# Attention scores: masks, scale and row minimum of the negated scores in one VectorE instruction per 128 columns, in place of two instructions per 512

## The chip, the cores and the metric

One Trainium2 chip, one core of it. The time is that of one execution on the device in microseconds (us); the kernel before was timed in three runs, and one more execution of it was profiled. Lower is better.

## What is computed

Three layers in a row: attention with a local window and global tokens, a gated feed-forward layer, and a soft mixture of experts. All data is float32. The change touches the first layer only, and there the local queries:

```python
def _attn_ref(q_l, k_l, v_l, q_g, k_g, v_g):          # B, H, Sl, D = 4, 8, 512, 64; Sg = 32
    pos = np.arange(Sl)
    window, scale = 32, 1.0 / np.sqrt(D)
    k_all = np.concatenate([k_g, k_l], axis=2)
    v_all = np.concatenate([v_g, v_l], axis=2)
    s_g = scale * np.matmul(q_g, k_all.transpose(0, 1, 3, 2))
    out_g = np.matmul(sm(s_g), v_all)                  # sm: softmax over the last axis, with its max taken off
    s_ll = scale * np.matmul(q_l, k_l.transpose(0, 1, 3, 2))
    mask = np.abs(pos[:, None] - pos[None, :]) <= window
    s_ll = np.where(mask, s_ll, -1e9)
    s_lg = scale * np.matmul(q_l, k_g.transpose(0, 1, 3, 2))
    a_l = sm(np.concatenate([s_lg, s_ll], axis=-1))
    out_l = np.matmul(a_l, np.concatenate([v_g, v_l], axis=2))
    return np.concatenate([out_g, out_l], axis=2)
```

Then `x = (silu(x @ w_gate) * (x @ w_val)) @ w_out`, and a soft mixture of eight experts of four slots each over the 2176 tokens.

## The kernel before

**Tiling of the attention.** A block of 32 local queries sees at most three blocks of 32 keys and the 32 global keys, so a window of 128 keys. `kS` holds the keys so that each window is 128 columns in a row. The work is cut into 16 units `u`: eight groups `n` of four heads (a batch and half of its heads), each in two parts `tp` of 256 queries. In one unit `stage_scores` (L328) does two halves `hp`. A half is eight matmuls (L342) into one PSUM tile `sc` of 128 partitions x 4 pieces `bp` x 128 columns: a row is one query of one head, and a piece is its window. Then VectorE works on the whole tile of 512 columns: one SCALAR_TENSOR_TENSOR (L351) multiplies by the scale and adds `masks`, into the SBUF tile `sm`, and one TENSOR_REDUCE (L355) takes the maximum of each row of each piece, negated, into the four columns of `nm`:

```python
nc.vector.scalar_tensor_tensor(
    out=sm, in0=sc, scalar=SCALE, in1=masks[:, 4 * tp : 4 * tp + 4],
    op0=ALU.mult, op1=ALU.add,
)
nc.vector.tensor_reduce(
    out=d["nm"][:, hp], in_=sm, op=ALU.max, axis=AX.X, negate=True
)
```

`stage_exp` (L359) runs one ScalarE instruction per piece (L363): exp of `sm` with the column of `nm` as bias, into `p`, and the sum of the row out of ScalarE's accumulator into `rs`. The accumulator is read by an instruction of its own, ACTIVATION_READ_ACCUMULATOR.

**The masks** are built once at the start: two triangles `tri` by GpSimd (L277, L281), filled with `NEG` = -1e9 outside, copied to the places of `masks`, and two memsets (L309, L311).

**The order of the work** is written out by hand: the kernel turns the scheduler off, so every engine does its instructions in the order of the program. The loop over `u` (L511) issues, in this order: the scores of `u`; `split_rest` (the low part of an earlier unit's output, L405 on VectorE); one piece of the preparation of the next layer's weights (`prep_some`, L137 to L157 on VectorE, from u = 5 on); the transposes `ppT` of `p` of unit u-1 on TensorE (L372) and their copy `pT` by ScalarE (L375); the exps of `u`. For tp = 0 follow the scores of the global queries `gs`, `gt` (L445), their maximum (L449 to L452) and exps (L458 to L465); for tp = 1 the transposes `pg` of `pG` (L475). Then `stage_pv` of u-1: `o` (L386), 1/sum (L393, L394) and the product `xn` (L396). For tp = 1 the second half of `pg` and its copy `pGT` by VectorE (L479). For tp = 0 `stage_gpv` of n-1: `og` (L491), the sums (L496 to L498) and `xg` (L503). For tp = 1 `turn_v` of n+1: three GpSimd copies (L248 to L250) that make two of the three orders of the values, `vB` and `vC`, out of `vA`. Then `stage_xT` of u-2 (L419, and its copy L403 by ScalarE). At the end of a tp = 0 step SyncE issues the loads of the next group's values (`load_v`, L228 on); they write the buffers that `og` and `o` of the group before have read, so they wait for these.

**Buffers around the change.** The scores, and the global scores, take turns in three PSUM buffers (`ps_sc`); `sm` has two buffers, one per half, so the scores of a unit are worked on when the exps of the unit before have read theirs.

After the attention the same weights' preparation goes on beside the gated layer (L587 on), which is a long row of matmuls, and the mixture of experts follows.

Of the kernel before, what the change touches and what calls it, by code (L numbers as in the profile page):

```python
# [12 lines left out]
ALU = mybir.AluOpType  # L13
AX = mybir.AxisListType
PSUM = bass.MemoryType.PSUM

NEG = -1e9
# [19 lines left out]
def window(i):  # L37

    if i == 0:
        return 0, "A", 0  # L40
    m, k = divmod(i - 1, 3)
    return (4 * m, 4 * m + 2, 4 * m + 3)[k], "ABC"[k], m
# [3 lines left out]
def attention_moe_soft_moe_kernel(  # L46
# [15 lines left out]
    nc = tc.nc  # L62
# [6 lines left out]
    SCALE = 1.0 / float(D) ** 0.5  # L69
# [124 lines left out]
    masks = ast.tile([P, 8, P], F32, name="masks")  # L194
# [57 lines left out]
    def spread_q(n, a, eng, xs=slice(0, 16)):  # L252

        rows = slice(64 * a, 64 * a + 64)
        dst = qB[n % 2][rows].rearrange("p (a x g) -> p a x g", a=2, g=64)[
            :, :, xs, 32 * a : 32 * a + 32
        ]
        src = qT[n][rows].rearrange("p a (x q) -> p a x q", q=32)[:, :, xs]
        if eng is nc.scalar:
            nc.scalar.activation(dst, src, AF.Copy)  # L260
        else:
            eng.tensor_copy(dst, src)
# [7 lines left out]
    for _ in range(2):  # L270
# [5 lines left out]

    nc.gpsimd.affine_select(  # L277
        out=tri[:, 0], in_=tri[:, 0], pattern=[[1, 32]], compare_op=ALU.is_ge,
        fill=NEG, base=0, channel_multiplier=-1,
    )  # L280
    nc.gpsimd.affine_select(  # L281
        out=tri[:, 1], in_=tri[:, 1], pattern=[[-1, 32]], compare_op=ALU.is_ge,
        fill=NEG, base=0, channel_multiplier=1,
    )
    nc.gpsimd.memset(qB[0], 0.0)
    warm = ast.tile([1, 1], F32, name="warm")
# [2 lines left out]
    for g in (0, 1, 3, 2):  # L289
        bl = g // 2  # L290
        eng = nc.gpsimd if g == 3 else nc.vector
        if g == 2:
            spread_q(0, 0, nc.vector, slice(0, 8))
            for a, x0 in ((1, 0), (1, 8), (0, 8)):
                spread_q(0, a, nc.scalar, slice(x0, x0 + 8))
        rows = masks[32 * g : 32 * g + 32]
        for r in range(3):
            first = next(i for i in range(1, 16) if i % 3 == r and i % 2 == bl)
            p0 = first // 2
            n = len(range(p0, 8, 3))  # L300
            k = window(first)[1]
            for a, slot in ((0, {"A": 1, "B": 0, "C": 0}[k]), (1, 3)):
                eng.tensor_copy(
                    rows[:, p0 :: 3, 32 * slot : 32 * slot + 32],
                    tri[:, a].unsqueeze(1).to_broadcast([32, n, 32]),
                )
        if bl == 0:
            eng.tensor_copy(rows[:, 0, 64:96], tri[:, 1])
            eng.memset(rows[:, 0, 96:128], NEG)  # L309
        else:  # L310
            eng.memset(rows[:, 7, 96:128], NEG)  # L311
    nc.gpsimd.memset(qgB, 0.0)
    make_identity(nc, ident)
    for a in range(2):
        rows = slice(64 * a, 64 * a + 64)
# [12 lines left out]
    def stage_scores(u):  # L328
        n, tp = units[u]
        st[u] = d = {  # L330
            "p": [awk.tile([P, 4, P], F32, tag=f"p{a}", name=f"p{u}_{a}") for a in range(2)],
            "rs": awk.tile([P, 4, 2], F32, tag="rs", name=f"rs{u}", bufs=4),
            "nm": awk.tile([P, 2, 4], F32, tag="nm", name=f"nm{u}"),
            "sm": [awk.tile([P, 4, P], F32, tag="sm", name=f"sm{u}_{a}") for a in range(2)],
        }
        qb = qB[n % 2].rearrange("p (a x g) -> p a x g", a=2, g=64)
        for hp in range(2):
            sc = ps_sc.tile([P, 4, P], F32, tag="sc", name=f"sc{u}_{hp}")
            for i in range(8):
                blk = 8 * tp + i  # L340
                s0 = window(blk)[0]
                nc.tensor.matmul(  # L342
                    sc[64 * (i % 2) : 64 * (i % 2) + 64, i // 2],
                    qb[:, hp, blk],
                    kS[n][:, hp, 32 * s0 : 32 * s0 + 128],
                    start=True, stop=True, skip_group_check=True,
                )
            if hp == 0 and tp == 1:
                split_rest()
            sm = d["sm"][hp]  # L350
            nc.vector.scalar_tensor_tensor(  # L351
                out=sm, in0=sc, scalar=SCALE, in1=masks[:, 4 * tp : 4 * tp + 4],
                op0=ALU.mult, op1=ALU.add,
            )
            nc.vector.tensor_reduce(  # L355
                out=d["nm"][:, hp], in_=sm, op=ALU.max, axis=AX.X, negate=True
            )

    def stage_exp(u):  # L359
        d = st[u]  # L360
        for hp in range(2):
            for bp in range(4):
                nc.scalar.activation(  # L363
                    d["p"][hp][:, bp], d["sm"][hp][:, bp], AF.Exp,
                    bias=d["nm"][:, hp, bp : bp + 1], accum_out=d["rs"][:, bp, hp : hp + 1],
                )

    def stage_pT(u, hp):
# [39 lines left out]
    def split_rest():  # L408
        while rest:
            rest.pop(0)()  # L410
# [100 lines left out]
    for u in range(NU):  # L511
        n, tp = units[u]
        stage_scores(u)
        split_rest()
        prep_some()
        if u >= 1:
            stage_pT(u - 1, 0)
            stage_pT(u - 1, 1)
        stage_exp(u)
        if tp == 1 and n + 2 < NQ:  # L520
            load_k(n + 2)
# [32 lines left out]
    for a in range(4):  # L554
        rows = slice(32 * a, 32 * a + 32)
        nc.gpsimd.tensor_copy(istack[rows], ident[rows, rows])
    nc.gpsimd.memset(isel, 0.0)
    for a in range(2):
        rows = slice(64 * a, 64 * a + 64)
# [108 lines left out]
    nm = tpool.tile([P, 4, 4], F32, name="nm")  # L668
# [228 lines left out]
    base = S1 * NFC  # L897
# [106 lines left out]
    d, a, b, top, turned, tokens, sums, NJ = part_end(2, Ls, [Ls], [place["rB"]])  # L1004
# [93 lines left out]
    for e in range(E):  # L1098
# [8 lines left out]
        out=lr, in0=lr, in1=rc[:, 0].unsqueeze(2).to_broadcast([P, NK * 4, NS]), op=ALU.subtract  # L1107
# [6 lines left out]
        out=lr, in0=lr, in1=rc[:, 1].unsqueeze(2).to_broadcast([P, NK * 4, NS]), op=ALU.mult  # L1114
    )
    nc.vector.transpose(
        out=cT.rearrange("p k n -> p (k n)"), in_=Lr.rearrange("p k n -> p (k n)")
# [151 lines left out]
```

## Time and profile before

| | us |
|---|---|
| median of three runs | 548.22 |
| lowest and highest of the three | 546.24, 549.87 |
| the profiled execution | 550.9 |
| span of its trace | 549.1 |
| TensorE busy in the span | 502.9 (92%) |
| VectorE busy | 327.6 (60%) |
| ScalarE busy | 182.8 (33%) |
| GpSimd busy | 83.4 (15%) |

The profile is of one execution. Its span is the time from the first to the last instruction; the 1.8 us between the span and the execution's own time lie around it. Busy time is a mean over stages which differ; the attention takes about the first 135 us.

In the profile PE is TensorE, PEld its weight loads, DVE VectorE, ACT ScalarE, POOL GpSimd, SP SyncE. A row of a timeline gives the start, the duration, the engine, the line, the operation, what it writes and reads, and shapes as partitions x elements.

### The profile page before, as it was taken

To read this page: it belongs to the slowest core of one execution; us is meant where nothing else is said; L and a number is where in the kernel's file an instruction comes from. 1 tells how busy PE (TensorE), PEld (TensorE's weight loads), DVE (VectorE), ACT (ScalarE), POOL (GpSimd) and SP (SyncE) were. 2 spreads that over 40 slices of the span, in tenths; PEclk is the share of its full clock that TensorE was granted. 3 is DMA by queue.
4 is the path that set the end of the run, shared out by engine and by line. 5 is a ranking of instruction groups with operands and counts; after the bars stand their busy time and mean duration, and the time that the engine had idled before them with its cause. 6 is when DMAs were issued, how large, how long until landed. Compare 5 with 4: busy or idle time off the path is not lost.

```text
span 549.1 us, 12632 instructions
## 1 busy us (share of the span) xinstructions
PE 502.9 (92%) x5274; PEld 373.6 (68%) x5274; DVE 327.6 (60%) x641; ACT 182.8 (33%) x550; POOL 83.4 (15%) x94
## 2 busy tenths in 40 slices
PE   5679889889999999999999999999999999969992
PEld 3568667768777777777777777776599998433631
DVE  8468999998876766776676677444143434512022
ACT  5458788785322322222232222112101102100011
POOL 7054345350201110010011101000000000010000
PEclk9779999999999999999999999999999999989996
DMA  8998678520454444444444454224099995869996
GB/s 218 247 238 240 193 216 244 163 73 20 154 175 146 168 146 153 156 153 135 136 166 143 150 199 164 97 78 154 4 341 391 412 411 206 308 218 344 348 358 210
DMA packets 62832, 110.81 MB, mean 202 GB/s; under 512 B 3800, under 2 KB 48696, under 8 KB 60856
## 3 DMA queue, kind: packets, MB, share of 16 engines
q1 hardware_dynamic: 62776, 110.02, 61.4%
q8 instruction: 41, 0.67, 0.5%
q14 instruction: 15, 0.12, 0.1%
HBM read 89.82 MB, written 20.19 MB: 200 GB/s over the span
## 4 chain that ended last, share of the span: by engine, by line
PE 61%; issue 13%; DVE 11%; DMA 5%; ACT 5%; SPq 3%; DVEq 0%; ACTq 0%
PE pval L587 22%; PE pgate L587 21%; PE T L749 3%; PE psh L1090 3%; SPq L865 2%; DMA f<-in_w_dram 2%; PE ppT L372 2%; DMA vC<-in_vl_dram 2%; DVE nm L355 2%; DMA qT<-in_qT_dram 2%; DVE sm L351 2%; PE sc L342 1%; PE o L386 1%; PE L L658 1%; ACT p L363 1%
## 5 line engine op out<-in xcount | busy, mean ns | idle before, releaser
L587 PE MATMUL pval<-x,w 128*128 128x512 f32 x432 | 112.2, 400 | 0.0
L587 PE MATMUL pgate<-x,w 128*128 128x512 f32 x432 | 109.7, 398 | 0.0
L587 PEld LDWEIGHTS pval<-x,w 128*128 128x128 f32 x432 | 79.3, 188 | 28.2 <-issue 11.6
L587 PEld LDWEIGHTS pgate<-x,w 128*128 128x128 f32 x432 | 79.4, 188 | 16.7
L602 DVE SCALAR_TENSOR_TENSOR u<-u,pgate 128x512 f32<-128x512 f32 (+2 forms) x60 | 36.5, 608 | 83.6 <-ACT u L601 83.5
L601 ACT ACTIVATE u<-pgate 128x512 f32<-128x512 f32 (+2 forms) x60 | 31.8, 530 | 128.1 <-PE pgate L587 106.3
L611 DVE SCALAR_TENSOR_TENSOR u<-u,pval 128x512 f32<-128x512 f32 (+2 forms) x60 | 36.4, 607 | 48.9 <-PE pval L587 48.8
L172 POOL TENSOR_TENSOR w<-wb,w 128x512 fp32r<-128x512 f32 x24 | 31.3, 1303 | 200.1 <-ACT w L171 173.9
L363 ACT ACTIVATE p<-sm,nm 128x128 f32<-128x128 f32 x128 | 49.5, 391 | 3.3 <-DVE nm L355 3.2
L587 PE MATMUL pgate<-x,wr 128*128 128x384 f32 (+1 forms) x288 | 49.4, 314 | 0.0
L587 PEld LDWEIGHTS pgate<-x,wr 128*128 128x128 f32 x288 | 43.5, 188 | 8.4 <-issue 7.4
L587 PE MATMUL pval<-x,wr 128*128 128x384 f32 (+1 forms) x288 | 48.4, 313 | 0.0
L587 PEld LDWEIGHTS pval<-x,wr 128*128 128x128 f32 x288 | 43.1, 188 | 7.0 <-issue 7.0
L171 ACT ACTIVATE w<-wb 128x512 fp32r<-128x512 f32 x24 | 15.2, 632 | 87.3 <-issue 51.3
L342 PE MATMUL sc<-kS,qB 128*64 128x128 f32 x512 | 34.3, 283 | 8.1 <-issue 2.7
L342 PEld LDWEIGHTS sc<-kS,qB 128*64 128x64 f32 x512 | 28.4, 140 | 13.8 <-issue 7.7
L157 DVE SCALAR_TENSOR_TENSOR wb<-wv,wb 128x512 f32<-128x512 f32 x36 | 25.9, 720 | 3.5
L614 DVE STREAM_TRANSPOSE hT<-u 128x512 f32<-128x512 f32 x36 | 25.6, 712 | 1.6 <-DVE u L611 0.4
L375 ACT ACTIVATE pT<-ppT 128x512 f32<-128x512 f32 x32 | 17.5, 595 | 26.1 <-PE ppT L372 26.1
L143 DVE SCALAR_TENSOR_TENSOR wb<-raw,wb 128x512 uint32<-128x512 uint32 x36 | 24.9, 692 | 1.1
L372 PE MATMUL ppT<-ident,p 128*128 128x128 f32 x128 | 18.4, 288 | 6.7 <-DVE pGT L479 6.7
L351 DVE SCALAR_TENSOR_TENSOR sm<-sc,masks 128x512 f32<-128x512 f32 x32 | 21.9, 683 | 4.4 <-PE sc L342 3.4
(209 smaller groups left out, 679.4 us busy)
## 6 DMA issues: line engine op xcount, KB each, us to landing
e<-in_w_dram SPq DMA_DIRECT2D x7, 2048.0 KB, 13.4
w_d<-w SPq DMA_DIRECT2D x24, 512.0 KB, 2.6
wr<-w_d SPq DMA_DIRECT2D x12, 1024.0 KB, 6.4
f<-in_w_dram SPq DMA_DIRECT2D x10, 1024.0 KB, 12.1
raw<-in_wgate_dram SPq DMA_DIRECT2D x12, 512.0 KB, 3.5
raw<-in_wval_dram SPq DMA_DIRECT2D x12, 512.0 KB, 3.9
raw<-in_wout_dram SPq DMA_DIRECT2D x12, 512.0 KB, 3.4
kS<-in_kS_dram SPq DMA_DIRECT2D x7, 736.0 KB, 6.7
```

Of the source, the lines that this page charges most:

```text
L143: nc.vector.scalar_tensor_tensor(out=d["t"], in0=d["raw"][:, :, 0], scalar=29, in1=d["t"], op0=ALU.logical_shift_right, op1=ALU.bitwise_or,)
L157: nc.vector.scalar_tensor_tensor(out=w, in0=d["v"], scalar=F64_NORMAL, in1=w, op0=ALU.is_ge, op1=ALU.mult)
L172: nc.gpsimd.tensor_tensor(out=wl, in0=w, in1=wh, op=ALU.subtract)
L342: nc.tensor.matmul(sc[64 * (i % 2) : 64 * (i % 2) + 64, i // 2], qb[:, hp, blk], kS[n][:, hp, 32 * s0 : 32 * s0 + 128], start=True, stop=T ...
L351: nc.vector.scalar_tensor_tensor(out=sm, in0=sc, scalar=SCALE, in1=masks[:, 4 * tp : 4 * tp + 4], op0=ALU.mult, op1=ALU.add,)
L363: nc.scalar.activation(d["p"][hp][:, bp], d["sm"][hp][:, bp], AF.Exp, bias=d["nm"][:, hp, bp : bp + 1], accum_out=d["rs"][:, bp, hp : hp + 1],
L372: nc.tensor.transpose(pt[:, bp], d["p"][hp][:, bp], ident)
L587: nc.tensor.matmul(ps[:, :n], w[:, 2 * k + a, cc * P : cc * P + P], xt[b][:, cc], start=(cc == 0 and i == 0), stop=(cc == NC - 1 and i == 2),)
L601: nc.scalar.activation(u[:, :n], pg[:, :n], AF.Tanh, scale=0.5)
L602: nc.vector.scalar_tensor_tensor(out=u[:, :n], in0=u[:, :n], scalar=1.0, in1=pg[:, :n], op0=ALU.add, op1=ALU.mult)
L611: nc.vector.scalar_tensor_tensor(out=u[:, :n], in0=u[:, :n], scalar=0.5, in1=pv[:, :n], op0=ALU.mult, op1=ALU.mult)
L614: nc.vector.transpose(out=hT[blk][:, c], in_=u[:, :n])
```

## The change

The mask values are divided by the scale (`NEG / SCALE`), since the mask is now added before the scaling. The two instructions per half are replaced by a loop over the four pieces: one `tensor_tensor_reduce` each, which computes `sm = (sc + masks) * -SCALE` and leaves the minimum of the row (from 3e38) in `nm`. `sm` so holds the negated scores, the minimum of them is the negated maximum, and the exp takes `scale=-1.0`.

```diff
         out=tri[:, 0], in_=tri[:, 0], pattern=[[1, 32]], compare_op=ALU.is_ge,
-        fill=NEG, base=0, channel_multiplier=-1,
+        fill=NEG / SCALE, base=0, channel_multiplier=-1,
     )
...
-            eng.memset(rows[:, 0, 96:128], NEG)
+            eng.memset(rows[:, 0, 96:128], NEG / SCALE)
...
             sm = d["sm"][hp]
-            nc.vector.scalar_tensor_tensor(
-                out=sm, in0=sc, scalar=SCALE, in1=masks[:, 4 * tp : 4 * tp + 4],
-                op0=ALU.mult, op1=ALU.add,
-            )
-            nc.vector.tensor_reduce(
-                out=d["nm"][:, hp], in_=sm, op=ALU.max, axis=AX.X, negate=True
-            )
+            for bp in range(4):
+                nc.vector.tensor_tensor_reduce(
+                    out=sm[:, bp], in0=sc[:, bp], in1=masks[:, 4 * tp + bp], scale=-SCALE,
+                    scalar=3e38, op0=ALU.add, op1=ALU.min,
+                    accum_out=d["nm"][:, hp, bp : bp + 1],
+                )
...
                 nc.scalar.activation(
                     d["p"][hp][:, bp], d["sm"][hp][:, bp], AF.Exp,
-                    bias=d["nm"][:, hp, bp : bp + 1], accum_out=d["rs"][:, bp, hp : hp + 1],
+                    bias=d["nm"][:, hp, bp : bp + 1], scale=-1.0, accum_out=d["rs"][:, bp, hp : hp + 1],
                 )
```

On VectorE, in unit 6 (tp = 0), the program before has these rows from the 1/sum of unit 4 (`ri4`, L393) over the copy `pGT` of the global probabilities (L479) to `split_rest` (L405); `sm6_0` and `sm6_1` are the two halves:

```order
L393 TENSOR_SCALAR ri4_890<-rs4_641 128x8
L394 RECIPROCAL ri4_890<-ri4_890 128x8 [waits DVE_49]
L396 TENSOR_TENSOR xn4_893<-o4_857,ri4_890 128x512 [waits DVE_49,PE_49]
L479 COPY pGT2_851<-pg2_3_895 128x384 [waits PE_49]
L351 SCALAR_TENSOR_TENSOR sm6_0_913<-sc6_0_915,masks_110 128x512 [waits PE_49,Activation_49]
L355 TENSOR_REDUCE nm6_912<-sm6_0_913 128x4 [waits DVE_49]
L351 SCALAR_TENSOR_TENSOR sm6_1_914<-sc6_1_926,masks_110 128x512 [waits PE_49,Activation_49]
L355 TENSOR_REDUCE nm6_912<-sm6_1_914 128x4 [waits DVE_49]
L405 TENSOR_TENSOR x0_82<-pxT3_903,x0_82 128x2x256 [waits Activation_49]
```

In the changed kernel, whose lines behind the change are one lower, the same place reads so. Each piece is two instructions of VectorE, the second of which only writes one column of `nm`:

```order
L392 TENSOR_SCALAR ri4_914<-rs4_657 128x8
L393 RECIPROCAL ri4_914<-ri4_914 128x8 [waits DVE_49]
L395 TENSOR_TENSOR xn4_917<-o4_881,ri4_914 128x512 [waits DVE_49,PE_49]
L478 COPY pGT2_875<-pg2_3_919 128x384 [waits PE_49]
L352 ISA sm6_0_937,nm6_936<-sc6_0_939,masks_110 128x128 [waits PE_49,Activation_49]
L352 ISA nm6_936 128x1
L352 ISA sm6_0_937,nm6_936<-sc6_0_939,masks_110 128x128
```

The pair stands four times for each half, 16 rows in place of 4 for a unit. The two waits of the reductions for the instruction before them (DVE) are gone, and no wait stands inside a half. On ScalarE the exps stand where they stood. Before, at the start of the program (unit 0, the exps of its two halves and the first of the global scores), the first exp of a half waits and the other three follow:

```order
L363 ACTIVATE p_0_201,rs_203<-sm_0_205,nm_204 128x128 [waits DVE_49]
L363 ACTIVATE p_0_201,rs_203<-sm_0_205,nm_204 128x128 x3
L363 ACTIVATE p_1_202,rs_203<-sm_1_206,nm_204 128x128 [waits DVE_49]
L363 ACTIVATE p_1_202,rs_203<-sm_1_206,nm_204 128x128 x3
L458 ACTIVATE pG,grs_251<-gs_238,gm_246 128x5x96 [waits DVE_49,PE_49,Pool_49]
```

and now each of the four has a wait of its own, for its piece:

```order
L362 ACTIVATE p_0_201,rs_203<-sm_0_205,nm_204 128x128 [waits DVE_49] x4
L362 ACTIVATE p_1_202,rs_203<-sm_1_206,nm_204 128x128 [waits DVE_49] x4
L457 ACTIVATE pG,grs_255<-gs_242,gm_250 128x5x96 [waits DVE_49,PE_49,Pool_49]
L461 ACTIVATE pG,grs_255<-gs_242,gm_250 128x32
L464 ACTIVATE pG,grs_255<-gt_243,gm_250 128x32 [waits PE_49]
```

So nothing moved there; the waits are for pieces now. No other instruction of any engine changes its place.

## Rows read from the trace of the kernel before

**Rows 1.** The page's slices of DVE (each 13.7 us, busy tenths).
```profile
DVE  8468999998876766776676677444143434512022
```

**Rows 2.** Busy time by window: five turns of the loop over groups, then the end.
```profile
core 0: us, PE busy (x) PEld busy (x) DVE busy (x) ACT busy (x) POOL busy (x), PEclk, DMA share, GB/s
49.00:62.00 13.00, 11.41 (x275) 9.41 (x276) 12.46 (x25) 10.94 (x45) 5.70 (x5) 1.00 0.73 202
62.00:77.00 15.00, 12.28 (x305) 9.91 (x293) 14.27 (x32) 11.31 (x47) 5.96 (x5) 1.00 0.68 212
77.00:90.00 13.00, 12.28 (x287) 9.81 (x284) 12.23 (x32) 11.48 (x46) 6.88 (x6) 1.00 0.85 243
90.00:104.00 14.00, 12.16 (x284) 10.07 (x285) 13.28 (x29) 11.74 (x50) 6.11 (x5) 1.00 0.58 150
104.00:119.00 15.00, 11.89 (x283) 9.62 (x282) 14.23 (x32) 11.44 (x46) 6.85 (x14) 1.00 0.60 160
119.00:140.00 21.00, 20.75 (x296) 17.05 (x296) 16.73 (x43) 13.04 (x43) 0.18 (x1) 1.00 0.14 40
```

**Rows 3.** The chain that ended last, unit 7: start, us, what.
```profile
66.68 0.61 DVE sm L351
...
68.64 0.69 DVE nm L355
69.32 1.02 DVE wb L149
70.34 1.16 DVE ri L393
```

**Rows 4.** Timeline of DVE, unit 6: start, us.
```profile
57.67 0.55 DVE L479 COPY pGT<-pg 128x384 f32<-128x384 f32 x1
58.13 0.68 DVE L351 SCALAR_TENSOR_TENSOR sm<-sc,masks 128x512 f32<-128x512 f32 x1
58.85 0.69 DVE L355 TENSOR_REDUCE nm<-sm 128x4 f32<-128x512 f32 x1
59.45 0.68 DVE L351 SCALAR_TENSOR_TENSOR sm<-sc,masks 128x512 f32<-128x512 f32 x1
60.17 0.69 DVE L355 TENSOR_REDUCE nm<-sm 128x4 f32<-128x512 f32 x1
60.77 0.68 DVE L405 TENSOR_TENSOR x<-pxT,x 128x512 fp32r<-128x512 f32 x1
...
62.98 0.15 DVE L452 TENSOR_SCALAR gm<-gm 128x1 f32<-128x1 f32 x1
63.05 0.16 DVE L393 TENSOR_SCALAR ri<-rs 128x8 f32<-128x8 f32 x1
```

**Rows 5.** Groups by line of DVE, shapes apart: a 128-column copy from PSUM.
```profile
L636 DVE COPY ws<-pwp 128x128 f32<-128x128 f32 x12 | 3.4, 283 | 0.0
```

**Rows 6.** Timeline of ACT, the first exps of unit 6.
```profile
60.02 0.39 ACT L363 ACTIVATE p<-sm,nm 128x128 f32<-128x128 f32 x1
60.31 0.19 ACT L363 ACTIVATION_READ_ACCUMULATOR p<-sm,nm 128x1 f32 x1
60.40 0.39 ACT L363 ACTIVATE p<-sm,nm 128x128 f32<-128x128 f32 x1
```

**Rows 7.** Timeline of PE, unit 6: the transposes of p, and og.
```profile
58.36 1.06 PE L372 MATMUL ppT<-ident,p 128*128 128x128 f32 x8 [1.29 <-DVE pGT L479]
...
61.43 0.74 PE L491 MATMUL og<-vA,pGT 128*32 128x64 f32 x40
```

**Rows 8.** Timeline of SP: the first load of the next values.
```profile
62.24 0.34 SPq L228 DMA_DIRECT2D vA<-in_vl_dram  x1
```

**Rows 9.** Timeline of POOL, unit 7: first and last copy of turn_v.
```profile
67.45 1.26 POOL L248 COPY vB<-vA 64x1280 f32<-64x1280 f32 x1 [8.57 <-DMA vA<-in_vl_dram]
...
69.86 1.60 POOL L250 COPY vC<-vA 32x1280 f32<-32x1280 f32 x1
```

**Rows 10.** Timeline of DVE, unit 7: the 1/sum beside that copy.
```profile
70.27 1.22 DVE L393 TENSOR_SCALAR ri<-rs 128x8 f32<-128x8 f32 x1
```

More of the change, by code (lines that the diff above doesn't have):

```diff
@@ L282, in attention_moe_soft_moe_kernel @@
         out=tri[:, 1], in_=tri[:, 1], pattern=[[-1, 32]], compare_op=ALU.is_ge,
-        fill=NEG, base=0, channel_multiplier=1,
+        fill=NEG / SCALE, base=0, channel_multiplier=1,
     )
@@ L308, in attention_moe_soft_moe_kernel @@
             eng.tensor_copy(rows[:, 0, 64:96], tri[:, 1])
-            eng.memset(rows[:, 0, 96:128], NEG)
+            eng.memset(rows[:, 0, 96:128], NEG / SCALE)
         else:
-            eng.memset(rows[:, 7, 96:128], NEG)
+            eng.memset(rows[:, 7, 96:128], NEG / SCALE)
     nc.gpsimd.memset(qgB, 0.0)
```

## The prediction

> **What bounds the kernel now.** I read the page's slices first. VectorE is busy nine tenths and more from the fifth slice to the ninth, some 55 to 123 us [rows 1], and less before and behind. So the change, which touches VectorE in the attention alone, has a stage in which it can count and others in which it can't.
>
> Then the windows, one for each turn of the loop over groups (two units; a turn ends where `og` ends and the next loads of values go out). In the five turns from 49 to 119 us VectorE is busy 12.46 of 13, 14.27 of 15, 12.23 of 13, 13.28 of 14 and 14.23 of 15 us [rows 2]: 94 to 96%. TensorE has 11.4 to 12.3 us in a turn and ScalarE 10.9 to 11.7. From 119 us on TensorE has 20.75 of 21 us and is the bound.
>
> Third the chain of waits: in unit 7 it runs through VectorE alone, over both halves of the scores, then the weight piece L149 with 1.02 us and the little 1/sum L393 with 1.16 us [rows 3].
>
> Last the timelines. Four instructions on the scores take 2.64 us of a unit: from the first L351 at 58.13 to L405 at 60.77 [rows 4]. A reduction that waits for the product before it starts 0.72 us behind it (58.13 to 58.85); an instruction that waits for nothing starts 0.60 us behind one of 512 columns that itself lasts 0.69 (58.85 to 59.45). So without a wait the next one starts some 0.09 us before the last one's end.
>
> **The change part by part.** *Removed:* in each half one product and one reduction over 512 columns, 1.32 us by the starts (58.13 to 59.45), in each unit 2.64 us [rows 4].
>
> *Added:* in each half four pairs, a main instruction over 128 columns and one that writes the accumulator, none with a wait for the other. No row shows either of them on VectorE. The main one is bounded by its neighbours: a copy of 384 columns is followed after 0.46 us (57.67 to 58.13), a reduction of 512 after 0.60 [rows 4], so 0.14 us for 128 columns, and 128 columns by the same line 0.60 - 3 x 0.14 = 0.18 us. From the other side it is the whole duration of a copy of 128 columns from PSUM, 0.283 us [rows 5], if the next one waited for its end. The read-out writes one column: an instruction of one column is followed after 0.07 us (62.98 to 63.05) [rows 4], and has 0.15 us as a whole. ScalarE does the same pair already: its read-out starts at 60.31, when the exp of 60.02 with its 0.39 us is not over, and the next exp starts 0.09 us behind it [rows 6]. So the pair costs 0.18 + 0.07 = 0.25 us at the least and 0.283 + 0.15 = 0.43 us at the most. I take 0.18 + 0.09 = 0.27, since ScalarE's rows are the nearest to such a pair and show no wait between the two. Eight pairs: 2.16 us, against 2.64: **0.48 us less for a unit**. By the bounds it is 0.64 less to 0.80 more (8 x 0.43 = 3.44). The point of indifference is 2.64 / 8 = 0.33 us for a pair.
>
> [...]
>
> [...]
>
> *What of it is on the path.* The scores of units 5 to 14, ten units, lie in the five turns. 10 x 0.48 = 4.8 us less on an engine that is at 94 to 96%. Not all of it comes out: the turn from 77 to 90 us has VectorE, TensorE and ScalarE at 12.23, 12.28 and 11.48 of 13 us [rows 2], and I count a third of its 0.96 us, so 0.6 us off. Unit 4 and the early ones add something where VectorE is in the chain now and then; I add 0.3 for them. Sum: -4.8 + 0.6 - 0.3 = **-4.5 us**. Units 0 to 3 lie where VectorE has idle time (4 and 6 tenths, [rows 1]), and unit 15 behind 119 us under TensorE; both count as nothing.
>
> *The exps* can start when their own piece is done, not when the whole half is. That is worth nothing while ScalarE is busy before: in unit 6 it starts its first exp at 60.02 [rows 6], though the first reduction of 58.85 with 0.69 us was over at 59.54. Four waits in place of one for a half cost nothing as long as a pair (0.27) is shorter than an exp with its read-out (0.38, 60.02 to 60.40); with 0.43 ScalarE would run at VectorE's pace for these pieces.
>
> *The PSUM buffers:* a half's scores are now read until its last pair, 4 x 0.27 = 1.08 us behind the start where it was 0.68. The buffer is wanted next by the global scores `gt`, behind the transposes of 58.36 to 59.42 [rows 7], so 0.2 us or more of cover are left; with 0.43 for a pair it would be read until 59.85, and the cover would have to come from `gs`. *The mask values* and *the sign in the exp* are constants in instructions that stand there anyway: nothing.
>
> *A stall that goes, and what is late next.* The 1/sum on 8 columns takes 1.22 us at 70.27 [rows 10] and 0.16 at 63.05 [rows 4]; in between GpSimd makes its three copies, 67.45 to 71.46 [rows 9], and the long one ends as the last copy ends. So some small VectorE instructions wait out a GpSimd copy, and the start of the copies hangs on a load that goes out when `og` is done (61.43, then 62.24 [rows 7, 8]), not on VectorE's scores: the transposes before `og` were waiting for `pGT`, which stands ahead of the scores of unit 6 [rows 7]. A VectorE that comes 0.48 us earlier may just wait longer for the same copy, or slip in a copy earlier and win 1.1 us at once. With copies one behind the other and arrivals at any phase, the mean of it is the time saved, and that is what I count.
>
> **The rivals.** *First, slower: the read-out waits until its main instruction is through, and the next main one for the read-out.* Then a pair is 0.43, a unit 0.80 longer, ten units 8.0 us: 548.2 + 8.0 = 556.2. It decides from 0.33 us for a pair on. For it: no row of VectorE shows a pair, and 12 instructions more for a unit have to be dispatched. Against it: the starts of VectorE without a wait [rows 4] and ScalarE's pair [rows 6].
>
> *Second, nothing comes out:* the copies of GpSimd and the load before them set the turn, and VectorE only waits longer at L393. For it: the end of L393 falls on the end of a copy [rows 9, 10], and the way from `pGT` by TensorE and the load to the copies has no scores in it. Against it: L149 and L393 would have to meet the same copy again in every turn, and the copies leave room between them. It gives -1.5 to 0 us, 547.5.
>
> *Third, more:* VectorE gets ahead of the copies in most turns, and the waits (some 0.4 us at L149 and 1.06 at L393 in a turn such as unit 7's [rows 3, 10]) go too. Four turns (all but the one from 77 on) with 1.1 us each on top of the 4.5: -8.9, 539.3. Against it: the turns are then at 13 us, where all three engines are nearly full.
>
> That the kernel would not do what the change says can be left out but for one point: "one instruction per 128 columns" is two in the program's order, and that is in the sum.
>
> **How the numbers follow.** The profiled execution has 550.9 us (span 549.1 and 1.8 around it); with -4.5 it would be 546.4. The median of the runs is 548.2, 2.7 below it, and the result is measured as a median: 548.2 - 4.5 = **543.7 us**. Chances: the forecast 0.50 (-2 to -7: 541 to 546.5), the first rival 0.20, the second 0.17, the third 0.13. The range reaches from 538.5 (the third rival's time, a little below) to 554, where a pair takes 0.40 us of the 0.33 to 0.43 of the first rival (548.2 + 10 x (8 x 0.40 - 2.64) = 553.8); what lies above is most of that rival. A measurement of this kernel tells about 1%, 5.5 us, from no change (its three runs lie 3.6 us apart). Faster by over 1%, below 542.7: the third rival and two fifths of the forecast, 0.13 + 0.19 = 0.32. Slower by over 1%, above 553.7: the part of the first rival with a pair above 0.40, 0.18 of its 0.20. The rest, 0.50, is within 1%.
>
> **What would show it right or wrong.** In the changed kernel's timeline of VectorE: the distance from one main instruction to the next in a half (0.27 expected; 0.33 indifferent; 0.43 the first rival), and the way from a unit's first one to L404 (2.16). In the windows: VectorE's busy time for a turn down by about 1 us. In the chain: still VectorE with 1/sum between 50 and 119 us, the turns 0.9 us shorter in the mean. If the pairs measure 0.27 and the end of the attention has not moved, the second rival holds; if L393 is back at 0.16 us in all turns, the third. The forecast is wrong if the main instructions lie 0.33 us apart or more, or if something behind 119 us moves by more than the shift.

## The result and the profile after

The changed kernel takes 544.18 us (median of 7 runs, 542.82 to 545.06), the kernel before 549.72 in 7 runs beside it (546.24 to 552.2): a ratio of 0.9898 with a 95% interval of 0.9872 to 0.9923. So it is 5.5 us faster. The profiled execution took 543.96 us with a span of 542.1, against 550.9 and 549.1: 7 us between these two single executions, of which one is a little above its median and one at it.

The timeline of DVE in unit 6, the place of [rows 4], with one row of start, duration, line and operation each:

```profile
55.95 0.55 DVE L478 COPY pGT<-pg 128x384 f32<-128x384 f32 x1
56.52 0.29 DVE L352 CUSTOM_DVE_ANT_0 sm<-sc,masks 128x128 f32<-128x128 f32 x1
56.74 0.08 DVE L352 DVE_READ_ACCUMULATOR2_ANT nm<- 128x1 f32 x1
56.74 0.28 DVE L352 CUSTOM_DVE_ANT_0 sm<-sc,masks 128x128 f32<-128x128 f32 x1
56.95 0.08 DVE L352 DVE_READ_ACCUMULATOR2_ANT nm<- 128x1 f32 x1
...
58.22 0.08 DVE L352 DVE_READ_ACCUMULATOR2_ANT nm<- 128x1 f32 x1
58.22 0.69 DVE L404 TENSOR_TENSOR x<-pxT,x 128x512 fp32r<-128x512 f32 x1
```

The pair is there, a main instruction and its read-out, but the next main one starts in the same hundredth of a microsecond as the read-out: 56.74 and 56.74. From one main instruction to the next it is 0.21 us, and the eight pairs of the unit take 58.22 - 56.52 = 1.70 us, where the four instructions before took 2.64 [rows 4]. That is 0.94 us less for a unit, twice what I had worked out. The groups of instructions by line, with shapes apart, give the same of all units (busy us, mean ns of one):

```profile
L352 DVE CUSTOM_DVE_ANT_0 sm<-sc,masks 128x128 f32<-128x128 f32 x128 | 28.6, 286 | 8.2 <-PE sc L342 7.4 <-issue 0.8
...
L352 DVE DVE_READ_ACCUMULATOR2_ANT nm<- 128x1 f32 x128 | 10.6, 83 | 0.0
```

A main instruction lasts 286 ns, as long as the copy of 128 columns [rows 5]; the next one starts 0.07 us before its end.

The windows, with a turn of the loop over groups in each row, as in [rows 2]:

```profile
49.00:61.00 12.00, 12.00 (x285) 10.05 (x285) 11.56 (x51) 11.19 (x46) 5.61 (x5) 1.00 0.75 221
61.00:74.00 13.00, 11.39 (x268) 9.21 (x269) 12.40 (x55) 10.18 (x43) 5.97 (x5) 1.00 0.80 241
74.00:87.00 13.00, 12.74 (x315) 10.56 (x304) 11.77 (x58) 12.44 (x52) 6.89 (x6) 1.00 0.86 245
87.00:100.00 13.00, 11.76 (x264) 9.51 (x266) 11.53 (x54) 11.53 (x50) 5.96 (x5) 1.00 0.66 173
100.00:113.00 13.00, 12.94 (x318) 10.82 (x306) 12.01 (x55) 10.74 (x43) 7.02 (x14) 1.00 0.64 171
113.00:134.00 21.00, 20.70 (x299) 17.53 (x297) 15.40 (x52) 12.64 (x41) 0.08 (x1) 1.00 0.14 41
```

The five turns now lie in 64 us, where they lay in 70. VectorE (the third number with its count) has come down from 12.2 to 14.3 us in a turn to 11.5 to 12.4. TensorE (the first) has 11.4 to 12.9 us, in the five turns together 60.8 us where it had 60.0: the same work in shorter turns, and now as much as VectorE's. The last row is the end under TensorE, which is busy for 20.7 of 21 us there, as before.

From the gated layer on hardly anything moved. Its first matmuls, in the kernel before and then in the changed one:

```profile
125.19 3.00 PE L587 MATMUL pgate<-x,w 128*128 128x512 f32 x12
```

```profile
118.88 3.00 PE L586 MATMUL pgate<-x,w 128*128 128x512 f32 x12
```

From there to the end of the span it is 423.9 us before and 423.2 now. So 6.3 of the 7 us between the two executions lie ahead of the gated layer.

The page's chain, by engine, of the kernel before and then of the changed one, shows the hand-over:

```profile
PE 61%; issue 13%; DVE 11%; DMA 5%; ACT 5%; SPq 3%; DVEq 0%; ACTq 0%
```

```profile
PE 64%; issue 13%; ACT 7%; DVE 6%; DMA 6%; SPq 3%; DVEq 0%; ACTq 0%
```

VectorE's share of the chain goes from 11 to 6%, some 27 us of the span; most of it did not vanish but went to TensorE and ScalarE, which were close behind.

Where a turn ends can be read from the first load of the next values, L228 on SP. Of the kernel before, the one that closes three turns after that of [rows 8], at 62.24:

```profile
104.17 0.45 SPq L228 DMA_DIRECT2D vA<-in_vl_dram  x1
```

and of the changed kernel the same two:

```profile
60.69 0.34 SPq L228 DMA_DIRECT2D vA<-in_vl_dram  x1
...
100.41 0.34 SPq L228 DMA_DIRECT2D vA<-in_vl_dram  x1
```

Three turns took 41.93 us before and take 39.72 now: 13.98 and 13.24 us for one. VectorE saved 1.88 us in each (two units), and 0.74 us came out. Over all five turns it is more, 70 us against 64, so 1.2 us for one. The stretch before the first of these turns hangs on loads (two of them alone are 36% of the chain up to 49 us in the kernel before and 38% in the changed one) and ends at a different time in each execution (44.66 to 51.96 us over all profiles), so I compare the profiles of all runs by these three turns. They are a rough measure: two profiles of the changed kernel and the run a_late, which has the same work, give 39.72, 38.98 and 38.22 us. The busy times in the three turns, of the kernel before and then of the changed one:

```profile
62.24:104.17 41.93, 36.64 (x854) 29.81 (x850) 39.70 (x91) 34.47 (x140) 18.95 (x16) 1.00 0.70 201
```

```profile
60.69:100.41 39.72, 36.61 (x851) 29.91 (x847) 36.28 (x168) 34.87 (x144) 18.82 (x16) 1.00 0.77 220
```

VectorE was busy for 95% of them and is now for 91; TensorE goes from 87 to 92% with the same work.

### The profile page after: what moved, and what is told of

It reads as the page before. It is cut to its first block, busy times and chain, and to the rows that moved or that the text cites. A ratio compares the mean times of both kernels' runs of the same rounds, so it can differ in the third digit from the quotient of the medians.

```text
span 542.1 us, 12820 instructions
## 1 busy us (share of the span) xinstructions
PE 503.6 (93%) x5274; PEld 374.6 (69%) x5274; DVE 315.7 (58%) x833; ACT 181.8 (34%) x550; POOL 83.3 (15%) x94
## 4 chain that ended last, share of the span: by engine, by line
PE 64%; issue 13%; ACT 7%; DVE 6%; DMA 6%; SPq 3%; DVEq 0%; ACTq 0%
PE pval L586 22%; PE pgate L586 22%; PE sc L342 3%; PE T L748 3%; PE psh L1089 3%; SPq L864 2%; ACT p L362 2%; DMA f<-in_w_dram 2%; PE ppT L371 2%; DMA vA<-in_vg_dram 2%; DMA kS<-in_kS_dram 2%; PE o L385 1%; PE L L657 1%; ACT woT L625 1%; DVE sm L352 1%
## 5 line engine op out<-in xcount | busy, mean ns | idle before, releaser
L352 DVE CUSTOM_DVE_ANT_0 sm<-sc,masks 128x128 f32<-128x128 f32 x128 | 28.6, 286 | 8.2 <-PE sc L342 7.4
L362 ACT ACTIVATION_READ_ACCUMULATOR p<-sm,nm 128x1 f32 x128 | 24.8, 194 | 0.0
```

The costliest lines, as they stand in the source:

```text
L352: nc.vector.tensor_tensor_reduce(out=sm[:, bp], in0=sc[:, bp], in1=masks[:, 4 * tp + bp], scale=-SCALE, scalar=3e38, op0=ALU.add, op1=ALU.min,
L362: nc.scalar.activation(d["p"][hp][:, bp], d["sm"][hp][:, bp], AF.Exp, bias=d["nm"][:, hp, bp : bp + 1], scale=-1.0, accum_out=d["rs"][:, b ...
```

## The experiments

Three theories were put against each other. **Theory 1:** the gain is VectorE's time, less than in proportion since the other engines are near full. **Theory 2:** the gain is that each exp waits only for its own piece. **Theory 3:** the gain is a shift of VectorE against GpSimd's copies, for which some of its instructions wait (the third rival's mechanism: L393 with 1.22 us beside a copy and 0.16 without one, [rows 10, 4]).

**a_pad: VectorE's time given back.**

```diff
                     accum_out=d["nm"][:, hp, bp : bp + 1],
                 )
+            nc.vector.tensor_reduce(out=padt, in_=sm[:, 0:3], op=ALU.max, axis=AX.X)
```

> The changed kernel with one more VectorE reduction over 384 columns of sm behind each half, into a scratch tile: 0.46 us by the starts, so VectorE's time for a unit goes from 1.70 back to 2.62 us (2.64 before), while the exps are still released piece by piece. Theory 1 (the gain is VectorE's time): the gain goes, 548.5 to 550.5 us. Theory 2 (the gain is that an exp waits for its own piece only): it stays, 543.5 to 545. Theory 3 (the gain is a shift against GpSimd's copies): in between, with the waits of 1/sum as long as before.

Measured: 549.27 us (12 runs), a ratio of 1.0009 to the kernel before (0.9985 to 1.0033). The timeline of DVE in its unit 8 (tp = 0 as in unit 6) shows the size of the pad:

```profile
74.76 0.28 DVE L353 CUSTOM_DVE_ANT_0 sm<-sc,masks 128x128 f32<-128x128 f32 x1
...
75.60 0.55 DVE L358 TENSOR_REDUCE padt<-sm 128x3 f32<-128x384 f32 x1
...
77.37 0.68 DVE L406 TENSOR_TENSOR x<-pxT,x 128x512 fp32r<-128x512 f32 x1
```

From 74.76 to 77.37 a unit has 2.61 us, where the kernel before had 2.64. The gain is gone, all of it, with the pieces still released one by one. That speaks for theory 1 and against theory 2.

**a_late: the early release taken away.**

```diff
         for hp in range(2):
-            for bp in range(4):
+            for bp in (3, 2, 1, 0):
                 nc.scalar.activation(
```

> The changed kernel with the exps of a half in the order of pieces 3, 2, 1, 0, so the first of them waits for the last pair of its half; the work is the same. Theory 1: no change against the changed kernel, 543.5 to 545. Theory 2: the gain goes, 548 to 550. Theory 3: no change.

Measured: 543.87 us, ratio 0.9894 (0.9868 to 0.9920). Nothing is lost. In the timeline of ACT the reason stands as it stood in [rows 6]: the exps of unit 6 begin behind the copies pT, at 56.47, and by then the last pair of the first half is long done (55.40).

```profile
55.50 1.08 ACT L374 ACTIVATE pT<-ppT 128x512 f32<-128x512 f32 x2 [0.37 <-PE ppT L371]
56.47 0.40 ACT L362 ACTIVATE p<-sm,nm 128x128 f32<-128x128 f32 x1
```

Theory 2 falls.

**b_half: half the saving.**

```diff
+            if hp == 0:
+                for bp in range(4):
+                    nc.vector.tensor_tensor_reduce(
...
+            else:
+                nc.vector.scalar_tensor_tensor(
...
-                    bias=d["nm"][:, hp, bp : bp + 1], scale=-1.0, accum_out=d["rs"][:, bp, hp : hp + 1],
+                    bias=d["nm"][:, hp, bp : bp + 1], scale=(-1.0, 1.0)[hp], accum_out=d["rs"][:, bp, hp : hp + 1],
```

> The new way in the first half of each unit, the old two instructions in the second (with the mask values divided by the scale in both; they vanish in the exp either way). VectorE's time for a unit is 0.47 us down in place of 0.94. Theory 1: if the gain is in proportion, 547; if the other engines take the last part of it, more than half of the gain is there, 545 to 546. Theory 2: half the exps are released early, 547. Theory 3: anything between 544 and 550, by the phase.

Measured: 545.47 us, ratio 0.9932 (0.9911 to 0.9952). Of the 5.2 us between the kernel before beside it (549.07) and the run a_late, 3.6 are there with half the saving. By the medians the first half of the saved time is worth more than the second, as theory 1 has it; since the intervals of half and whole overlap, the times alone do not show it.

**a_noacc: the price of the read-out.**

```diff
-                    accum_out=d["nm"][:, hp, bp : bp + 1],
+                    accum_out=None,
...
-                    bias=d["nm"][:, hp, bp : bp + 1], scale=-1.0, accum_out=d["rs"][:, bp, hp : hp + 1],
+                    bias=zero, scale=-1.0, accum_out=d["rs"][:, bp, hp : hp + 1],
```

> The changed kernel without the read-out: the main instructions alone, and a constant 0 as the exp's bias in place of the minimum (the row's maximum is not taken off; the softmax is the same number without it). If the read-out costs nothing, the main instructions still start 0.21 us apart and the time is the changed kernel's, 543.5 to 545; if it costs its 0.08 us, they start 0.13 us apart, VectorE has 0.64 us less in a unit, and the time is 541 to 543.

Measured: 542.53 us, ratio 0.9886 (0.9863 to 0.9909). The timeline of DVE, where the eight main instructions of a unit are now one merged row:

```profile
54.30 1.67 DVE L353 CUSTOM_DVE_ANT_0 sm<-sc,masks 128x128 f32<-128x128 f32 x8
55.88 0.42 DVE L137 TENSOR_SCALAR wb<-raw 128x512 uint32<-128x512 uint32 x1
```

From 54.30 to 55.88 it is 1.58 us, 0.198 for one, against 1.70 and 0.2125 with the read-outs. A read-out costs 0.015 us on VectorE, not its 0.083. The time lies in the range that I had given for a read-out at its full 0.08 us, and near the changed kernel's: the two expectations lie too close together for the time alone to tell. The spacing tells it, and it speaks for almost no cost.

**b_noadd and a_noadd: the waits for GpSimd's copies.** In both kernels the sum of a row gets 1e-9 added (L393); it is at least 1, so nothing changes in float32 without it.

```diff
-        nc.vector.tensor_scalar_add(ri, d["rs"], 1e-9)
-        nc.vector.reciprocal(out=ri, in_=ri)
+        nc.vector.reciprocal(out=ri, in_=d["rs"])
```

> The kernel before without the addition of 1e-9 to the sum of a row (L393; the sum is at least 1, so float32 does not change by it): the reciprocal reads the sum itself. Theory 3 (the waits of that addition for GpSimd's copies, 1.1 us in four turns of five, are on the path): 544 to 546. Theory 1 (VectorE's time): 0.19 us of VectorE for a unit and what of the waits does not turn up at another instruction: 546 to 548. If the wait only moves to the reciprocal: 549 to 550.

> The same addition taken out of the changed kernel. Theory 3: 540 to 542. Theory 1: the engines are all near full there, so 542 to 543.5. If the wait only moves: 543.5 to 545.

Measured: 544.35 us for the kernel before without the addition, ratio 0.9917 (0.9886 to 0.9949), and 544.22 us for the changed one without it, 0.9899 (0.9859 to 0.9939). The changed kernel itself, run beside them, took 543.55 (0.9889, 0.9859 to 0.9918), for which the expectation was:

> The changed kernel once more, beside the three of this call: 543 to 545 by every theory.

So taking out sixteen tiny instructions, and with them the waits, wins the kernel before some 5.6 us, as much as the whole change; and on top of the change it wins nothing. The first lies in theory 3's range and below theory 1's. The second lies above the ranges of both, where I had put a wait that only moves. But the rows show that the wait does not move on. The timeline of DVE in b_noadd, unit 7:

```profile
63.91 1.55 DVE L149 SCALAR_TENSOR_TENSOR wb<-raw,wb 128x512 uint32<-128x512 uint32 x1
65.39 0.19 DVE L393 RECIPROCAL ri<-rs 128x8 f32<-128x8 f32 x1
```

The weight piece L149 still waits out a copy (1.55 us where 0.68 is its own), but the reciprocal does not: 0.19 us, though GpSimd copies at that time (64.98 to 66.37 and on). In the changed kernel the wait is there as before; the timeline of DVE, unit 7:

```profile
66.35 1.54 DVE L149 SCALAR_TENSOR_TENSOR wb<-raw,wb 128x512 uint32<-128x512 uint32 x1
67.81 1.01 DVE L392 TENSOR_SCALAR ri<-rs 128x8 f32<-128x8 f32 x1
```

So theory 3 is wrong for the change: its waits have stayed (1.01 and 1.54 us here). In all five turns the addition that can meet a copy lasts 1.22, 1.22, 0.16, 1.23 and 1.01 us before, and 1.24, 1.01, 0.79, 1.01 and 1.23 us in the changed kernel. And its mechanism is real: in the kernel before, these waits are a part of what makes VectorE the bound. The additions of the ten units take some 5.9 us up to the start of the reciprocal, waits included, and 5.6 us came out.

In a_noadd VectorE has room (busy for 32.34 of 38.83 us in the three turns), and two of the turns take 12.2 us. In the third, of 14.4, TensorE stands still in the global scores, without a wait that the profile shows ("issue"):

```profile
98.00 1.02 PE L443 MATMUL gs<-kS,qgB 128*64 128x480 f32 x5 [1.38 <-issue]
```

It stands in the global scores of the same turn in the two profiles of the changed kernel (0.85 and 0.84 us) and in a_late (1.66). What holds it there stays open.

**b_nomax and f_base: what is the next bound?** b_nomax is the kernel before with the reduction simply left out and a constant 0 as the bias; f_base takes out the addition of 1e-9 as well.

```diff
-            nc.vector.tensor_reduce(
-                out=d["nm"][:, hp], in_=sm, op=ALU.max, axis=AX.X, negate=True
-            )
...
-                    bias=d["nm"][:, hp, bp : bp + 1], accum_out=d["rs"][:, bp, hp : hp + 1],
+                    bias=zero, accum_out=d["rs"][:, bp, hp : hp + 1],
```

> The kernel before without the reduction: the old product over 512 columns alone, and a constant 0 as the exp's bias (the row's maximum is not taken off). VectorE has 1.2 us for a unit, 0.5 us less than in the changed kernel. Theory 1 with the other engines as the next bound: little beyond the changed kernel, 541.5 to 544. If VectorE were still the only bound: 539 to 540 (10 units x 0.5 us below it).

> Both reliefs of VectorE together: no reduction (constant 0 as the exp's bias, the row's maximum is not taken off) and no addition of 1e-9 to the sums. Theory 1 with a common floor of the other engines: 541.5 to 543.5, no better than either alone, and turns of the loop over groups of some 12.3 us, TensorE's own work in them. If VectorE and its waits for GpSimd were still the bound: 537 to 539.

Measured: 542.69 us for b_nomax (ratio 0.9879, 0.9835 to 0.9924) and 540.24 for f_base (0.9867, 0.9811 to 0.9923). f_base came out 1.3 us below the range that I had given for a common floor, with two of its six runs at 544; its interval covers those of the changed kernel and of b_nomax, so it is not shown to be faster than either. With 0.5 us less for a unit than the changed kernel, b_nomax would have been at 539 to 540 if VectorE alone were the bound. Its turns, by the loads on SP:

```profile
59.77 0.34 SPq L228 DMA_DIRECT2D vA<-in_vl_dram  x1
...
96.62 0.34 SPq L228 DMA_DIRECT2D vA<-in_vl_dram  x1
```

Three turns take 36.85 us, 12.28 each, and in its windows TensorE is busy 11.75 of 12 us:

```profile
61.00:73.00 12.00, 11.75 (x282) 9.70 (x280) 10.93 (x26) 10.61 (x46) 6.11 (x5) 1.00 0.82 262
```

The same three turns in the other runs: 42.39 us in a_pad, 40.08 in b_half, 38.22 in a_late, 38.98 in the second run of the changed kernel, 38.84 in b_noadd, 38.83 in a_noadd, 36.68 in a_noacc, 37.05 in f_base:

```profile
62.24:99.29 37.05, 35.97 (x852) 29.86 (x847) 28.92 (x68) 33.22 (x137) 18.92 (x16) 1.00 0.81 233
```

So with less and less work for VectorE the turns go from 14.0 us down to some 12.3 and no further, though in f_base VectorE is busy for only 78% of them. TensorE is busy for 97%. In two of f_base's three turns it waits before the scores for ScalarE's exps of the global queries, as here:

```profile
75.92 1.09 PE L343 MATMUL sc<-kS,qB 128*64 128x128 f32 x16 [0.25 <-ACT pG L459]
```

**f_act and f_pe: is it TensorE or ScalarE?** On top of f_base, one takes ScalarE's read-outs away (the reciprocal then reads a constant), the other half of TensorE's transposes.

```diff
-                    bias=zero, accum_out=d["rs"][:, bp, hp : hp + 1],
+                    bias=zero,
```

```diff
-        pt = ps_tr.tile([P, 4, P], F32, tag="tr", name=f"ppT{u}_{hp}")
-        for bp in range(4):
-            nc.tensor.transpose(pt[:, bp], d["p"][hp][:, bp], ident)
+        if hp == 0:
+            d["pt"] = ps_tr.tile([P, 4, P], F32, tag="tr", name=f"ppT{u}_{hp}")
...
+        pt = d["pt"]
```

> The same without the sums of the exps (128 read-outs of ScalarE's accumulator, 0.09 us each by the starts; the output is divided by 1 in place of the sum): 0.75 us of ScalarE less for a unit. If ScalarE is the floor: 4 to 7 us below the run with both reliefs. If TensorE is: within 1 us of it.

> Both reliefs, and only the first half's exps are transposed by TensorE (L372); ScalarE copies the same transposes for both halves, so the second half's probabilities do not enter the output. TensorE has 0.5 us less for a unit, ScalarE as much as before. If TensorE is the floor: 3 to 5 us below the run with both reliefs. If ScalarE is: within 1 us of it.

Measured: 540.18 us for f_act (ratio 0.9852, 0.9805 to 0.9900), the same as f_base; 544.26 for f_pe (0.9928, 0.9890 to 0.9966), 4 us above it, with intervals that overlap. By the medians ScalarE is not the floor (f_act), and less work for TensorE does not help (f_pe). The profiles tell more. From 49 to 110 us the windows have, for f_act and then f_pe:

```profile
49.00:110.00 61.00, 60.50 (x1422) 50.87 (x1421) 50.55 (x120) 49.28 (x150) 31.10 (x35) 1.00 0.73 209
```

```profile
49.00:110.00 61.00, 55.06 (x1353) 44.57 (x1353) 48.06 (x117) 54.92 (x227) 31.78 (x35) 1.00 0.75 209
```

Without the read-outs TensorE is busy 60.50 of 61 us, and in the three turns all of the time:

```profile
58.74:94.09 35.35, 35.35 (x851) 29.89 (x847) 29.99 (x70) 28.79 (x89) 18.81 (x16) 1.00 0.81 239
```

They are the shortest of all runs, 35.35 us or 11.8 for one. So there TensorE alone is the floor, and the 0.6 us for a turn that f_base has above it go with ScalarE's read-outs; the median does not show them. With fewer transposes TensorE and ScalarE have 55 us each, and the turns are no shorter (37.58 us for the three). There TensorE waits for ScalarE's copies pT before `o`, once in each of the three turns, as here, besides 0.83 us once for ScalarE's exps and 1.47 us with no wait that the profile shows:

```profile
62.05 0.32 PE L386 MATMUL o<-vA,pT 128*32 128x64 f32 x8 [0.42 <-ACT pT L375]
```

So by these rows TensorE and ScalarE hold the turns together: TensorE by its own work, ScalarE by the waits that it causes. Why f_pe's median lies above f_base's stays open, and these two profiles can't tell it: f_pe's is of its fastest execution (540.22 us), f_base's of its second slowest (543.76).

## Why the prediction was right

**The time.** Forecast 543.7 us, 4.5 less; measured 544.18, 5.5 less than before beside it. The sign, the stage and the engine were right: VectorE bound the five turns, and a_pad, which only gives VectorE its time back, loses the whole gain. The forecast that the chain would still run through VectorE failed: its share went from 11 to 6%, and TensorE and ScalarE took it over.

**The size of a pair was wrong by a quarter, and with it the saving by half.** The step "I take 0.18 + 0.09 = 0.27" failed in its second term: the main instruction was 0.198 us (a_noacc), between the 0.18 and the 0.283 of the bounds and near the lower, but the read-out 0.015, not the 0.07 or 0.09 that the nearest rows gave. Even the lower bound, 0.25 for a pair, was above the 0.2125 measured: an instruction of one column on VectorE and ScalarE's own read-out were no bound for it. So a unit saved 0.94 us in place of 0.48, and ten units 9.4.

**What comes out was wrong the other way.** "-4.8 + 0.6" let seven eighths of the saving through. Of the 9.4 us about 5.5 came out, so 3.9 are lost where I had put 0.6: this term is the one that was too small. I had set only one turn at the common floor. I had read the rows for the others ([rows 2]: TensorE 11.4 to 12.3 of 13 to 15 us), but applied them only to the turn which was at 13 us already. In two profiles of the changed kernel and that of a_late, five of the nine turns take 11.8 to 12.5 us, which is TensorE's own work with short waits. The other four take 13.7 to 14.2 us, and not all of that is VectorE either: in one TensorE waits for VectorE's `pGT`,

```profile
70.47 1.07 PE L371 MATMUL ppT<-ident,p 128*128 128x128 f32 x8 [1.27 <-DVE pGT L478]
```

and in three it stands in the global scores as in a_noadd. f_base shows the floor, with 97% of TensorE and 78% of VectorE in turns of 12.3 us; the medians of b_half (3.6 us for half the saving) and b_nomax (about 1 us for 0.5 us more in a unit) agree with it. The two errors worked against each other; the total was right partly by that luck.

**The 0.3 us for the units before** does not show. The load that opens the five turns goes out at 48.65 us before and at 48.82 now, and anywhere from 44.66 to 51.96 in the other profiles.

**The first rival** (the read-out waits until its main instruction is through) is refuted by the rows at 56.74: a main instruction of 286 ns is followed by the next one after 0.21 us.

**The second rival** (VectorE only waits longer for the copies) is refuted: the turns are 0.74 us shorter while the waits have stayed. **The third** (the waits go too) did not come about either: the addition is at 0.79 us and more in every turn. b_noadd speaks for its price: the waits of four turns come to 4.0 us there, and with the additions' own time 5.6 came out. On top of the change they would have won nothing, as a_noadd shows.

**The exps** were costed at nothing, and a_late agrees. **The PSUM buffers** had more cover than I gave them, as a half is read for 0.85 us (four times 0.2125), not 1.08.

## What to carry to other kernels

An accumulator output on VectorE is nearly free beside its main instruction here (0.015 us behind 0.198, a_noacc), so one pass with it beats a product and a reduction even when it must be cut into four pieces (1.70 us against 2.64 for a unit). The cut costs some 0.06 us a piece, as an estimate (four times 0.2125 us against 0.60 for one instruction of 512 columns); the second pass costs 0.60 us and the wait for the first, 0.12 us (0.72 from start to start in place of 0.60, [rows 4]). When three engines are each busy for most of a stage (here 95, 87 and 82% of the three turns before the change), count the saving on one only down to the work of the next in *every* turn, not in the shortest one. Look for tiny instructions with long durations before replacing large ones: in the kernel before, sixteen additions on 8 columns were worth 5.6 us (b_noadd), as much as the change.

## What was unexpected of the hardware

The read-out of VectorE's accumulator lasts 83 ns in the records and delays the next instruction by 15 ns (1.70 us for eight pairs against 1.58 for eight main instructions alone in a_noacc). ScalarE's own one is followed after 0.09 us [rows 6]. The one engine's row was no measure for the other.

Of VectorE's instructions some wait out a GpSimd copy here and some do not. The addition on 8 columns (1.22 us against 0.16, [rows 10, 4]) and the weight piece L149 with two sources in SBUF (1.55 against 0.68, b_noadd) wait. The reciprocal on the same 8 columns does not (0.19 in b_noadd), nor do the main instructions of the change, which read scores from PSUM and masks from SBUF: all 128 last 280 to 294 ns, though 50 of them start while a GpSimd copy runs. What sets the two kinds apart no run shows.
